# The last modulation vector of an adaLN block: one ScalarE scaling and a chain of accumulating DMAs in the place of VectorE sums and two matmuls

## The chip, the cores and the metric

The kernel runs on one core of one Trainium2 chip. The metric is the device time of one execution in microseconds (us). The kernel before ran three times: 440.43, 440.69 and 441.95 us, median 440.69 us. A separate execution was taken with the hardware profiler.

## The reference

One adaLN block on x of 2048 tokens by D = 448 channels, float32. Six modulation vectors of 448 numbers come from one matrix product; the last one, `gb`, is the subject of this document.

```python
mod = (_silu(c) @ w_mod).reshape(c.shape[0], 6, 1, -1)
sa, ca, ga, sb, cb, gb = (mod[:, 0], ..., mod[:, 5])
h = _layernorm(x) * (1 + ca) + sa
x = x + ga * _A_ref(h, A_wqkv, A_wo)        # linear attention, 16 heads of 28
h = _layernorm(x) * (1 + cb) + sb
x = x + gb * _B_ref(h, B_w1, B_b1, B_w2, B_b2)
```

`_B_ref` is a token-mixing MLP: layernorm, a product over the 2048 tokens with w1 (2048 by 1792), a gelu, and a product with w2 (1792 by 2048), each with a bias. `gb` multiplies what the MLP returns, so it is wanted only after the first of its two large products.

## The kernel before

**Layout.** Tokens are cut into 16 tiles of 128 rows (`NT`). Every float32 product is done as two or three fp32r matmuls: an operand is split into a high part (ScalarE copy) and a low part (VectorE subtraction, or a ScalarE negated copy followed by an accumulating DMA issued by GpSimd, as in `split_to`, `low` and `a_pk_parts`).

**Stages in program order.** After a start-up part, the loop `for t in range(3, NT)` (line 594) is the *first token stage*: for each token tile it projects keys, builds the high and low parts of phi(k), and adds to the 448 by 448 product `cacc` (line 453). Behind it stand the short middle parts: the sums `zs` and `zp` (lines 664 to 669), `csum`, `kvb` (line 691), `wp` (line 846) and the rows of `wp`, copied by SyncE DMAs (line 718). The loop `for i in range(NT + LAG)` (line 855) is the *second token stage*: it applies attention to tile i (`tq` line 758, `op` line 778), normalizes, and from i = 5 on runs the first steps of the w1 product (`up`, lines 828 to 830). The rest of the w1 product and the w2 product (`y`, lines 1028 and 1029) follow.

**Order and queues.** The schedule is written out by hand (`manual_schedule`): each engine runs its instructions in program order, so a waiting instruction holds up all that is behind it on the same engine. SyncE (SP) issues the loads in one such order, and GpSimd (POOL) issues the accumulating DMAs between its own small vector operations.

**Buffers.** Most tiles live in one pool of 76 buffers (`slot`, `NSLOT`); some in a pool of 25 (`tslot`, `NTOK`). A load whose buffer isn't free yet waits on SP, with all later loads behind it. Loads of w1 pieces (`pr`, `load_to`, line 242) run ahead of their splitting (`ph` and `pl`, `split_to`).

**The modulation vectors.** `sc` holds silu(c) as 112 rows by 4 columns. Vector j needs four tiles of w_mod (`load_mod`, line 113: 112 rows by 448), each scaled by one column of `sc`, added up, and then summed over the 112 rows. `mod_part` does the scaling and adding (ScalarE for the first piece of vector 5, line 179, VectorE for the other three, line 183). `mod_split` cuts the sum into high and low parts. `mod_sum2` multiplies both with a matrix of ones (lines 199 and 200), which sums over the rows and puts the result on all 128 partitions at once, and `mod_out` copies it out of PSUM (line 161).

For vector 5, `gb`, the four loads are issued at i = 12 of the second token stage, `mod_part` runs at i = 13, 14 and twice at 15, the matmuls at i = 16. Its readers come later: the multiplication of the gelu's result (`act`, line 945) and the bias term (lines 1155 and 1171).

Of the kernel before, what the change touches and what calls it, by code (L numbers as in the profile page):

```python
# [8 lines left out]
F32 = mybir.dt.float32  # L9
F32R = mybir.dt.float32r  # L10
AF = mybir.ActivationFunctionType
ALU = mybir.AluOpType
AX = mybir.AxisListType

P = 128
S, D, F = 2048, 448, 1792
NT = S // P
NF = F // P
G = 112
# [15 lines left out]
PRE2 = {16: (1, 0), 12: (1, 1), 8: (1, 2), 3: (4, 3), 1: (4, 4)}  # L35
MOD_AT = {11: [(4, 0)], 12: [(4, 1)], 13: [(4, 2)], 14: [(4, 3)], 15: [(3, 0), (3, 1)]}
QS = {0: 2, 4: 2}
WARM = 9
ACT_STATS = ()
PRE = 9  # L40
# [7 lines left out]
def block_kernel(ctx: ExitStack, tc: tile.TileContext, x, wqkv, wo, w1, b1, w2, b2, c, wmod, out):  # L48
    nc = tc.nc
# [5 lines left out]
    cst = ctx.enter_context(tc.tile_pool(name="cst", bufs=1))  # L55
# [9 lines left out]
    def slot(name, w=D, dt=F32, parts=P):  # L65
        return slots.tile([parts, w], dt, name=name, tag="slot", padded_shape=[P, 512])
# [41 lines left out]
    wm = {}  # L108

    def load_mod(j):  # L110
        for k in range(4):
            wm[j, k] = (tslot if j == 5 else slot)(f"wm{j}_{k}", parts=G)
            nc.sync.dma_start(wm[j, k], wmod[k * G:(k + 1) * G, j * D:(j + 1) * D])

    raw_w = {}
# [38 lines left out]
    nc.vector.tensor_scalar_add(ec, ec, 1.0)  # L154
    nc.vector.reciprocal(ec, ec)
    nc.vector.tensor_mul(sc, ct, ec)
    mods, macc, part = {}, {}, {}

    def mod_out(j, ps):
        mods[j] = cst.tile([P, D], F32, name=f"mod{j}")  # L160
        nc.scalar.activation(mods[j], ps[:, :D], AF.Copy, bias=1.0 if j in (1, 4) else 0.0)
# [13 lines left out]
    def mod_part(j, k):  # L175
        if k == 0:
            macc[j] = (tslot if j == 5 else slot)(f"acc{j}", parts=G)
            if j == 5:
                nc.scalar.activation(macc[j], wm[j, 0], AF.Copy, scale=sc[:, 0:1])
            else:  # L180
                nc.vector.tensor_scalar_mul(macc[j], wm[j, 0], sc[:, 0:1])
        else:
            nc.vector.scalar_tensor_tensor(macc[j], wm[j, k], sc[:, k:k + 1], macc[j], op0=ALU.mult, op1=ALU.add)
# [7 lines left out]
    def mod_split(j):  # L191
        acc = macc.pop(j)
        macc[j] = (moving(slot, f"mh{j}", parts=G), moving(slot, f"ml{j}", parts=G))
        split(acc, *macc[j])

    def mod_sum2(j):
        ps = bank(f"modp{j}")
        hi, lo = macc.pop(j)
        nc.tensor.matmul(ps[:, :D], ones_r[:G, :], hi, start=True, stop=False)
        nc.tensor.matmul(ps[:, :D], ones_r[:G, :], lo, start=False, stop=True)  # L200
        return ps

    Whi, Wlo = {}, {}

# [28 lines left out]
    raws, parts = {}, {}  # L233
    done = {"load": 0, "split": 0}

    def load_to(i):
        while done["load"] < min(i, len(pieces)):
            k = done["load"]
            src, r, c0, n = pieces[k]
            raws[k] = slot(f"pr{k}", 4 * P)  # L240
            rows = 1 if n == 4 else 2
            nc.sync.dma_start(raws[k].rearrange("p (r c) -> p r c", r=rows),
                              src[r * P:(r + rows) * P, c0 * P:(c0 + n) * P].rearrange("(r p) c -> p r c", p=P))
            done["load"] += 1

    def split_to(i):
        while done["split"] < min(i, len(pieces)):
            k = done["split"]
            if k in TOKP:
                hi, lo = tslot(f"ph{k}", F32R, w=4 * P), tslot(f"pl{k}", F32R, w=4 * P)  # L250
            else:
                hi, lo = slot(f"ph{k}", 4 * P, F32R), slot(f"pl{k}", 4 * P, F32R)
            if k in PIECE_DMA:
                full = raws.pop(k)
                nc.scalar.activation(hi, full, AF.Copy)
                nc.scalar.activation(lo, hi.bitcast(F32), AF.Copy, scale=-1.0)
                nc.gpsimd.dma_start(lo, full, accum_op=ALU.add)
            else:
                split(raws.pop(k), hi, lo)
            parts[k] = (hi, lo)  # L260
            done["split"] += 1
# [332 lines left out]
    for t in range(3, NT):  # L594
        kp = project(t, 1, "kp")
        if t + 1 < NT:
            a_transpose(t + 1)
        a_outer(t - KV_LAG)
        if t in Q_EARLY:
            a_q(t)  # L600
        if t == 10:
            mp = mod_sum2(2)
        if t + 1 < NT:
            a_split(t + 1)
        if t + 2 < NT:
            a_norm_a(t + 2)

        for j, i in MOD_AT.get(t, ()):
            mod_part(j, i)
        if 11 <= t < 15:  # L610
            nc.vector.tensor_mul(wo_sb[t - 11], wo_sb[t - 11], mods[2][:G])
        a_exp(t, kp)
        if t + 2 < NT:
            a_norm_b(t + 2)
        a_pk(t, kp)
        a_phi_q()
        a_pk_parts(t - 1)
        if t + 3 < NT:
            a_stats(t + 3)
        if t + 2 < NT:  # L620
            a_dup(t + 2)
        if t == 3:
            a_high(3)
            a_high(4)
        if t + 2 < NT:
            a_high(t + 2)
        if t == 10:
            mod_out(2, mp)
        if t + 4 < NT:
            load_x(t + 4)  # L630
        if 5 <= t < 9:
            mod_part(2, t - 5)
        if t == 9:
            mod_split(2)
        if 5 <= t <= 5 + QLATE:
            phi_q_sum(t - 5)
        if t in (10, 11):
            load_mod(14 - t)
        if t == 4:
            for g in range(4):  # L640
                w = tslot(f"wo{g}", parts=G)
                nc.sync.dma_start(w, wo[g * G:(g + 1) * G, :])
                wo_sb.append(w)
            load_qkv(2, tslot)
            b1c = cst.tile([P, NF], F32, name="b1c")
            nc.sync.dma_start(b1c, b1.rearrange("(k p) -> p k", p=P))
            b2c = cst.tile([P, NT], F32, name="b2c")
            nc.sync.dma_start(b2c, b2.rearrange("(k p) -> p k", p=P))
        load_to(PRE_LOAD.get(t, 0))
# [20 lines left out]
    mod_split(4)  # L670
    mod_split(3)
    load_to(14)
    split_to(4)
    zb = tslot("zb")
    nc.scalar.activation(zb, zp[:, :D], AF.Copy, bias=S * 1e-6)
# [18 lines left out]
    kvm = slot("kvm", parts=G)  # L694
    nc.vector.tensor_mul(kvm, kvb[:G, :D], mask)
    mod_out(4, mp)
    mp = mod_sum2(3)
    load_to(PRE + MID + 3)
    split_to(8)
# [104 lines left out]
    def b_mean2(t, i):  # L804
        nm2s[t] = small.tile([P, 1], F32, name=f"ny{t}", tag="ny")
        nc.gpsimd.tensor_scalar_mul(nm2s[t], sums.pop(t), -1.0 / D)
        b_square(ys[t], nm2s[t], b_sums(i)[:, 1:2], f"b{t}")
# [36 lines left out]
    for g in range(4):  # L844
# [5 lines left out]
        Wph.append(hi)  # L850
        Wpl.append(lo)
    mod_out(3, mp)

    accs, early = None, []
    for i in range(NT + LAG):
        if i == NT - 4:
            load_mod(5)
        if NT - 3 <= i < NT:
            mod_part(5, i - NT + 3)
        if i < NT:  # L860
            b_transpose(i)
        if 0 <= i - 1 < NT:
            b_out(i - 1)
        nq = min(len(late), QS.get(i, 1))
        for _ in range(nq):
            a_q(late.pop(0))
        t = i - LAG
        mp = mod_sum2(5) if i == NT else None
        if t >= 0:
            if t == 0:  # L870
                accs = [bank(f"up{f}") for f in range(4)]
            if i > NT:
                if not early:
                    early = [bank(f"up{W1G[1][0] + f}") for f in range(W1G[1][1])]
                r = i - NT - 1
                step(NT + r, early, H2h[r], H2l[r], r == 0, False)
            step(t, accs, H2h[t], H2l[t], t == 0, t == NT - 1)
        if mp is not None:
            mod_out(5, mp)
        scale, res, norm1, norm2 = i + 1 < NT, 0 <= i - 2 < NT, 0 <= i - 3 < NT, 0 <= i - 4 < NT  # L880
        if i < NT:
            b_high(i)
        if res:
            b_res(i - 2)
        if scale:
            b_prod(i + 1)
        if norm2:
            b_norm2(i - 4, i)
        if res:
            b_mean1(i - 2, i)  # L890
        if norm1:
            b_norm1_a(i - 3)
        if scale:
            b_sum(i + 1)
        if norm1:
            b_norm1_b(i - 3, i)
        if scale:
            b_eps(i + 1)
        if i < NT:
            b_low(i)  # L900
        if norm1:
            b_mean2(i - 3, i)
        if scale:
            b_recip(i + 1)
        if scale:
            b_scale(i + 1)
        if scale:
            b_dup(i + 1)
        if norm2:
            b_low2(i - 4)  # L910
        a_phi_q(nq)
        load_to(14 + (i + 1) // 2)
        if res or norm1:
            b_rstd(i, 0 if res else 1, 2 if norm1 else 1)
        if i == NT - 1:
            mod_part(5, 3)
            mod_split(5)
        split_to(10 + (i + 1) // 2)


# [291 lines left out]
```

## Time and profile before

| | |
|---|---|
| median of three runs | 440.69 us (440.43 to 441.95) |
| profiled execution, its own device time | 440.77 us |
| span of the profiled execution, first to last instruction | 439.1 us |
| PE (TensorE) busy in the span | 433.9 us, 99% |
| DVE (VectorE) busy | 365.1 us, 83% |
| ACT (ScalarE) busy | 266.9 us, 61% |
| POOL (GpSimd) busy | 119.3 us, 27% |
| granted TensorE clock | 1.0 throughout |

Times inside the execution are counted in us from the first instruction. The columns of a timeline are: start, duration, engine, line, operation, written tile <- read tiles, shapes, count, and in brackets the idle time of the engine before it with what ended it. "SPq" is the queue of DMA issues on SyncE. A row of the view of waits gives engine, line, what it waited for, then total us, number of waits and the longest. Matmuls overlap: a matmul's row lasts about 0.36 us, but the next one starts about 0.2 us after it, and that distance is what a matmul costs.

### The profile page before, as it was taken

The page shows a single profiled execution, that of the slowest core. Times are in us where ns is not written, and L with a number is a line of the kernel's source. Part 1 is how long each engine was busy: PE and PEld are TensorE (multiplying, and loading weights), DVE is VectorE, ACT ScalarE, POOL GpSimd, SP SyncE. Part 2 cuts the span into 40 slices and gives each one's busy share as a digit, 9 for nine tenths or more (in the row PEclk, how much of TensorE's full clock was granted, in tenths as well). Part 3 has the DMA queues.
Part 4 walks back from the last instruction along what each step waited for, and adds up shares of the span by engine and source line. Part 5 has one row for each costly group of instructions (what it writes and reads, how often), then busy time and mean ns, then how long its engine had stood idle before and what let it go on. Part 6 is the DMA issues. An engine that isn't in the chain of part 4 may idle for free.

```text
span 439.1 us, 7288 instructions
## 1 busy us (share of the span) xinstructions
PE 433.9 (99%) x2394; PEld 402.4 (92%) x2394; DVE 365.1 (83%) x792; ACT 266.9 (61%) x570; POOL 119.3 (27%) x196
## 2 busy tenths in 40 slices
PE   8999999999999999999999999999999999999996
PEld 7689999999899999999999999999999999999996
DVE  5996898988898999997469586439999998898894
ACT  3778877655657777776766254236675555655550
POOL 2205775520024455664300000010112230231110
PEclk9999999999999999999999999999999999999999
DMA  8987999993441224222427546476667977977531
GB/s 233 303 213 117 181 197 230 221 258 102 138 100 26 47 47 123 50 50 60 132 69 237 177 143 186 131 194 187 151 143 191 177 172 176 188 161 208 75 52 34
DMA packets 65022, 64.51 MB, mean 147 GB/s; under 512 B 8472, under 2 KB 56792, under 8 KB 64984
## 3 DMA queue, kind: packets, MB, share of 16 engines
q1 hardware_dynamic: 54608, 47.62, 36.8%
q0 software_dynamic: 10368, 16.42, 23.8%
q8 instruction: 19, 0.31, 0.3%
q14 instruction: 19, 0.16, 0.1%
q10 hardware_dynamic: 8, 0.00, 0.0%
HBM read 41.88 MB, written 7.34 MB: 112 GB/s over the span
## 4 chain that ended last, share of the span: by engine, by line
PE 95%; DMA 3%; DVE 1%; ACT 0%; issue 0%; SPq 0%; DVEq 0%
PE y L1028 19%; PE up L829 10%; PE up L828 10%; PE up L830 10%; PE y L1029 9%; PE op L778 8%; PE cacc L453 8%; PE qp L356 7%; PE kp L356 7%; DMA wl<-wr 2%; PE tq L758 2%; PE tp L325 1%; DMA wm<-in_w_mod_dram 1%; PE kvb L691 1%; PE wp L846 1%; PE colp L475 0%
## 5 line engine op out<-in xcount | busy, mean ns | idle before, releaser
L829 PE MATMUL up<-h2l,ph 128*128 128x448 f32 x224 | 81.3, 363 | 0.0
L828 PE MATMUL up<-h2h,ph 128*128 128x448 f32 x224 | 81.2, 362 | 0.0
L830 PE MATMUL up<-h2h,pl 128*128 128x448 f32 x224 | 80.7, 360 | 0.0
L988 POOL DMA_DIRECT2D a<-a x16 | 14.1, 948 | 145.5 <-DMA a<-in_B_w_dram 97.8
L828 PEld LDWEIGHTS up<-h2h,ph 128*128 128x128 f32 x224 | 42.0, 188 | 3.3
L830 PEld LDWEIGHTS up<-h2h,pl 128*128 128x128 f32 x224 | 41.9, 187 | 3.0
L829 PEld LDWEIGHTS up<-h2l,ph 128*128 128x128 f32 x224 | 42.0, 188 | 2.1
L80 DVE TENSOR_TENSOR pl<-pr,ph 128x512 fp32r<-128x512 f32 x48 | 32.3, 686 | 11.5 <-ACT ph L79 8.6
L79 ACT ACTIVATE ph<-pr 128x512 fp32r<-128x512 f32 x48 | 29.1, 627 | 17.8 <-PE up L829 7.4
L1050 ACT ACTIVATE cc<-y 128x448 f32<-128x448 f32 x24 | 13.0, 544 | 22.9 <-PE y L1029 22.9
L453 PE MATMUL cacc<-pkh,xh 128*128 128x448 f32 x64 | 24.3, 379 | 0.0
L453 PE MATMUL cacc<-pkl,xh 128*128 128x448 f32 x64 | 23.2, 363 | 0.0
L778 PE MATMUL op<-oh,pth 128*128 128x448 f32 x60 | 23.0, 383 | 0.0
L1071 POOL DMA_DIRECT2D out_dram<-yt x14 | 12.9, 921 | 34.9 <-DVE yt L1057 25.4
L778 PE MATMUL op<-oh,ptl 128*128 128x448 f32 x60 | 21.7, 362 | 0.0
L356 PE MATMUL qp<-wh,hh 128*128 128x448 f32 x60 | 21.6, 365 | 0.0
L356 PE MATMUL qp<-wh,hl 128*128 128x448 f32 x60 | 21.4, 362 | 0.0
L356 PE MATMUL kp<-wh,hl 128*128 128x448 f32 x56 | 20.3, 363 | 0.0
L356 PE MATMUL kp<-wh,hh 128*128 128x448 f32 x56 | 20.2, 362 | 0.0
L736 POOL TENSOR_SCALAR den<-den 128x16 f32<-128x16 f32 x16 | 8.6, 536 | 39.2 <-DVE den L733 39.1
L763 ACT ACTIVATE pth<-tq 128x512 fp32r<-128x512 f32 (+1 forms) x16 | 9.6, 599 | 15.7 <-PE tq L758 15.6
L302 POOL TENSOR_TENSOR rs<-ve,mhalf 128x1 f32<-128x1 f32 x16 | 13.9, 869 | 18.8 <-DVE ve L300 18.5
(234 smaller groups left out, 1356.9 us busy)
## 6 DMA issues: line engine op xcount, KB each, us to landing
pr<-in_B_w_dram SPq DMA_DIRECT2D x56, 256.0 KB, 2.9
a<-in_B_w_dram SPq DMA_DIRECT2D x32, 256.0 KB, 4.3
a<-in_B_w_dram SPq DMA_DIRECT2D x32, 192.0 KB, 4.2
wm<-in_w_mod_dram SPq DMA_DIRECT2D x24, 196.0 KB, 4.9
x<-in_A_x_dram SPq DMA_DIRECT2D x16, 224.0 KB, 4.0
out_dram<-x SPq DMA_DIRECT2D x14, 224.0 KB, 2.0
out_dram<-yt POOLq DMA_DIRECT2D x14, 224.0 KB, 4.5
pk<-pk POOLq DMA_DIRECT2D x12, 224.0 KB, 4.7
```

What stands on the lines that cost most here:

```text
L79: nc.scalar.activation(hi, full, AF.Copy)
L80: nc.vector.tensor_sub(lo, full, hi.bitcast(F32))
L302: nc.gpsimd.tensor_tensor(rs, ve, mhalf[:, 0:1], op=ALU.pow)
L356: nc.tensor.matmul(o, a[:, ch * P:(ch + 1) * P], b, start=(n == 0), stop=(n == 10))
L453: nc.tensor.matmul(cacc[ch][:, :D], a[:, s], b, start=(t == 0 and i == 0), stop=(t == NT - 1 and i == len(todo) - 1))
L778: nc.tensor.matmul(opb[t][:, :D], a[:, g * P:(g + 1) * P], b, start=(n == 0), stop=(n == len(todo) - 1))
L828: nc.tensor.matmul(ps[:, :D], hi[:, sl], mh, start=first, stop=False)
L829: nc.tensor.matmul(ps[:, :D], hi[:, sl], ml, start=False, stop=False)
L830: nc.tensor.matmul(ps[:, :D], lo[:, sl], mh, start=False, stop=last)
L988: nc.gpsimd.dma_start(w, a, accum_op=ALU.add)
L1028: nc.tensor.matmul(ps[:, :D], h[:, s], w, start=opens and r == r0, stop=False, skip_group_check=True)
L1029: nc.tensor.matmul(ps[:, :HD], l[:, s], wh, start=False, stop=closes and r == PAIRS - 1 - (LAST if (q, m) == (NP - 1, 6) else 0), skip_gro ...
```

## The change

- **Loads.** The four tiles of w_mod for vector 5 are loaded at t = 12 of the first token stage instead of i = 12 of the second, ahead of the w1 pieces of that place, and lie in the pool of 76 instead of the pool of 25.
- **Scaling.** ScalarE scales the four tiles in place: two at t = 14 and two at t = 15.
- **Sum.** Ten accumulating DMAs, all issued by GpSimd, do the additions. At t = 15 tile 2 is added to tile 0 and tile 3 to tile 1; after `mod_split(3)` tile 1 is added to tile 0. Then seven folds each add the lower half of the remaining rows to the upper half: 112 rows to 56 after `mod_out(4)`, 56 to 28 after `mod_out(3)`, and 28 to 14, 7, 4, 2 and 1 at i = 3 to 7 of the second token stage. Each needs the one before.
- **Spreading.** SyncE writes the one row to DRAM at i = 9 and reads it back onto all 128 partitions at i = 10.
- **Removed.** For vector 5: three VectorE multiply-adds, the split, two matmuls and their PSUM bank, and the ScalarE copy out of PSUM.

```diff
+FOLD_AT = {3: 28, 4: 14, 5: 7, 6: 4, 7: 2}
...
-            wm[j, k] = (tslot if j == 5 else slot)(f"wm{j}_{k}", parts=G)
+            wm[j, k] = slot(f"wm{j}_{k}", parts=G)
...
+    def mod_fold(j, n):
+        acc = macc[j]
+        h = (n + 1) // 2
+        nc.gpsimd.dma_start(acc[:n - h], acc[h:n], accum_op=ALU.add)
+
+    def mod_row(j):
+        mrow[j] = park.tile([1, D], F32, name=f"mrow{j}")
+        nc.sync.dma_start(mrow[j], macc.pop(j)[:1])
+
+    def mod_rows(j):
+        mods[j] = cst.tile([P, D], F32, name=f"mod{j}")
+        nc.sync.dma_start(mods[j], mrow[j].to_broadcast([P, D]))
...
+        if t == 12:
+            load_mod(5)
+        if t in (14, 15):
+            for k in (2 * t - 28, 2 * t - 27):
+                nc.scalar.activation(wm[5, k], wm[5, k], AF.Copy, scale=sc[:, k:k + 1])
+        if t == 15:
+            for k in range(2):
+                nc.gpsimd.dma_start(wm[5, k], wm[5, k + 2], accum_op=ALU.add)
...
     mod_split(3)
     load_to(14)
+    nc.gpsimd.dma_start(wm[5, 0], wm[5, 1], accum_op=ALU.add)
+    macc[5] = wm[5, 0]
...
     mod_out(4, mp)
+    mod_fold(5, G)
...
     mod_out(3, mp)
+    mod_fold(5, 56)
...
-        if i == NT - 4:
-            load_mod(5)
-        if NT - 3 <= i < NT:
-            mod_part(5, i - NT + 3)
...
-        mp = mod_sum2(5) if i == NT else None
...
-        if mp is not None:
-            mod_out(5, mp)
...
         if norm1:
             b_mean2(i - 3, i)
+        if i in FOLD_AT:
+            mod_fold(5, FOLD_AT[i])
+        if i == 9:
+            mod_row(5)
+        if i == 10:
+            mod_rows(5)
...
-        if i == NT - 1:
-            mod_part(5, 3)
-            mod_split(5)
```

More of the change, by code (lines that the diff above doesn't have):

```diff
@@ L156, in block_kernel @@
     nc.vector.tensor_mul(sc, ct, ec)
-    mods, macc, part = {}, {}, {}
+    mods, macc, part, mrow = {}, {}, {}, {}
     def mod_out(j, ps):
```

## The prediction

> **What bounds the kernel now.** I read the page first, then what PE waited for, then the busy time by stage.
>
> ```profile
> span 439.1 us, 7288 instructions
> PE 433.9 (99%) x2394; PEld 402.4 (92%) x2394; DVE 365.1 (83%) x792; ACT 266.9 (61%) x570; POOL 119.3 (27%) x196
> ...
> PE 95%; DMA 3%; DVE 1%; ACT 0%; issue 0%; SPq 0%; DVEq 0%
> ```
>
> ```profile
> PE warm L143 <- DVE mhalf L97: 1.1, 1, 1.1
> PE tp L489 <- DVE xn L515: 0.4, 1, 0.4
> ```
>
> ```profile
> 94.00:125.00 31.00, 31.00 (x170) 27.75 (x169) 25.52 (x46) 18.74 (x39) 0.81 (x3) 1.00 0.49 148
> 125.00:205.00 80.00, 80.00 (x426) 74.50 (x425) 74.88 (x179) 58.16 (x124) 44.20 (x91) 1.00 0.25 56
> 205.00:425.00 220.00, 220.00 (x1256) 207.94 (x1255) 177.48 (x376) 121.67 (x259) 30.83 (x43) 1.00 0.63 158
> ```
>
> The chain that ended last is 95% PE; PE's only two listed waits, 1.5 us in all, lie in the start-up; and in the three stages that the change touches PE is busy for the whole stretch. (Columns of the last fence: stretch, its length, then busy time and count of PE, weight loads, DVE, ACT and POOL, then the granted clock.) So TensorE's own stream sets the end. Taking work from PE shortens the run by what that work occupies; work taken from or given to other engines counts only once PE has to wait. The upside is therefore small and known, the downside is any new wait of PE.
>
> **The change part by part.** *Two matmuls go.*
>
> ```profile
> 203.78 0.37 PE L199 MATMUL modp<-mh,ones_r 112*128 112x448 f32 x1
> 203.98 0.37 PE L200 MATMUL modp<-ml,ones_r 112*128 112x448 f32 x1
> 204.19 0.37 PE L828 MATMUL up<-h2h,ph 128*128 128x448 f32 x1
> ```
>
> From the start of the first to the start of the next other matmul: 204.19 - 203.78 = 0.41 us. That is the whole gain on the path. The VectorE multiply-adds, the split and the copy out of PSUM that also go are hidden behind PE's full stretch; I count them as nothing.
>
> *Four scalings on ScalarE.* Two come at t = 14, two at t = 15. Their price is that of the same form at the start of the kernel, the L165 row; the timeline of ScalarE shows where they fall.
>
> ```profile
> L165 ACT ACTIVATE acc<-wm,sc x2: 668/668/668, 4.2 to 7.9; 112x448 f32<-112x448 f32 x2
> ```
>
> ```profile
> 94.45 0.55 ACT L363 ACTIVATE ek<-kp 128x448 f32<-128x448 f32 x1 [2.48 <-PE kp L356]
> ...
> 96.70 0.58 ACT L427 ACTIVATE pkh<-pk 128x448 fp32r<-128x448 f32 x1 [0.81 <-DVE pkl L429]
> 97.19 1.14 ACT L79 ACTIVATE ph<-pr 128x512 fp32r<-128x512 f32 x2
> ```
>
> The first two, 1.34 us, fit into the 2.48 us that ScalarE idles before 94.45. The last two start when it falls idle at 96.70 - 0.81 = 95.89 and end by 97.23, so `pkh` of the last tile comes up to 0.53 us late, and VectorE, which waits for it, hands that on to `zl`:
>
> ```profile
> 103.02 0.62 DVE L80 TENSOR_TENSOR zl<-pk,zh 128x448 fp32r<-128x448 f32 x1 [0.70 <-ACT zh L79]
> ```
>
> ```profile
> 105.45 0.36 PE L669 MATMUL zp<-zl,ones_r 128*128 128x448 f32 x1
> ```
>
> `zl` ends at 103.64, its matmul starts at 105.45: 1.81 us of cover against 0.53. Cost nothing; without that cover, 0.53.
>
> *Four loads move ahead of the w1 pieces.* SP issues one load when a buffer comes free, so the four take the places of four pieces.
>
> ```profile
> SPq L242 <- DMA xl<-h: 7.3, 1, 7.3
> ```
>
> ```profile
> 82.52 18.95 SPq L242 DMA_DIRECT2D pr<-in_B_w_dram  x14
> ...
> 89.53 1.40 SPq L242 DMA_DIRECT2D pr<-in_B_w_dram  x2
> ...
> 109.36 0.37 SPq L242 DMA_DIRECT2D pr<-in_B_w_dram  x1
> 115.56 0.57 SPq L718 DMA_DIRECT2D oh<-wph  x1
> 149.07 20.26 SPq L242 DMA_DIRECT2D pr<-in_B_w_dram  x3
> 169.38 1.83 SPq L113 DMA_DIRECT2D wm<-in_w_mod_dram  x4
> ```
>
> ```profile
> pr<-in_B_w_dram SPq DMA_DIRECT2D x56, 256.0 KB, 2.9
> wm<-in_w_mod_dram SPq DMA_DIRECT2D x24, 196.0 KB, 4.9
> pk<-pk POOLq DMA_DIRECT2D x12, 224.0 KB, 4.7
> pl<-pr POOLq DMA_DIRECT2D x8, 256.0 KB, 3.4
> wl<-wr POOLq DMA_DIRECT2D x1, 224.0 KB, 8.1
> oh<-wph SPq DMA_DIRECT2D x1, 28.0 KB, 2.3
> ```
>
> The first piece then goes out with the fifth issue, at 89.53, and lands 2.9 us later at 92.4; ScalarE wants it at 97.19. The w_mod tiles themselves, issued from 82.52 on and within the four places before 89.53, land 4.9 us after that, by 94.4 at the worst, and their scalings come at 92 to 96. Behind the last load of this group SP turns to the copies of `wp`, which wait for other work until 115.56; the group ended at 109.36 + 0.37, which leaves 5.8 us for the four places. The bound on the other side is the slot rival below. Later on 1.83 us of SP's time at 169.38 comes back, which nothing needed.
>
> *Ten accumulating DMAs on POOL.* The pair is issued behind the last scaling, at 97.23 and about 98.1, one issue costing about 0.94 us (L257, below). With the 4.7 us of the `pk` row it has landed at 102.8, the third at 107.5, and the fold of 112 rows is issued by 108.5. Behind it on POOL stands `den` of the first tile:
>
> ```profile
> 114.71 0.29 POOL L736 TENSOR_SCALAR den<-den 128x16 f32<-128x16 f32 x1 [23.05 <-DVE den L733]
> ...
> 159.30 0.23 POOL L806 TENSOR_SCALAR ny<-sy 128x1 f32<-128x1 f32 x1
> 160.40 0.19 POOL L811 TENSOR_SCALAR vw<-vs 128x2 f32<-128x2 f32 x1 [0.88 <-ACT sqb L285]
> ...
> 163.57 0.65 POOL L736 TENSOR_SCALAR den<-den 128x16 f32<-128x16 f32 x1 [0.24 <-DVE den L733]
> ```
>
> POOL idled 23.05 us there: 6.2 us of cover are left. Were every link as slow as the worst row, 8.1 us, that fold would be issued by 115.2 and `den` be 0.5 us late.
>
> The folds at i = 3 to 7 stand between `ny` and `vw`. At i = 7 POOL idles 0.88 us at that place and again 0.24 us before the `den` of a later tile, which `pn`, and then PE's transpose, wait for:
>
> ```profile
> L257 POOL DMA_DIRECT2D pl<-pr x8: 894/944/970, 126.5 to 203.5; - x8
> ```
>
> ```profile
> 165.54 0.20 DVE L751 COPY pn<-pn 128x64 f32<-128x64 f32 x1
> ```
>
> ```profile
> 161.10 0.27 PE L758 MATMUL tq<-ident,pn 128*128 128x128 f32 x1
> 166.16 0.38 PE L758 MATMUL tq<-ident,pn 128*128 128x128 f32 x2
> ```
>
> One issue of 0.94 us overruns the 0.88 by 0.06; cover behind that is 0.24 + (166.16 - 165.74) = 0.66 us. The fold before was issued one token step, 166.16 - 161.10 = 5.06 us, earlier, and needs 3.4 us to land by the row of the same stage. So: nothing, and small folds should be cheaper still.
>
> Here a rule speaks against the change. The Trainium skill (SBUF — State Buffer, section SBUF: two separate sides) says that a VectorE copy from SBUF to SBUF in fp32 keeps GpSimd from writing the descriptors of its DMAs, and gives about 3.1 us instead of 0.62 for one; by that difference, an estimate of 2.5 us from this page, each of the five folds could hold up POOL and the time would be some 9 us longer. This trace doesn't show it: eight issues in that stage, where VectorE is busy 94%, lie between 0.894 and 0.970 us, and the only such copy of a token step lasts 0.20 us.
>
> *The row and its spreading.* At i = 9 SP waits for the last fold (issued about 160.5, landed about 164), then 2.3 us for the write and up to 4.9 for the read: `gb` is there at about 171. It is first read at 224.9; the piece that queues behind the two on SP is read after 201.77.
>
> ```profile
> L945 DVE TENSOR_TENSOR u<-u,mod x14: 614/618/626, 224.9 to 314.8; 128x448 f32<-128x448 f32 x14
> ```
>
> ```profile
> 201.77 0.62 ACT L255 ACTIVATE ph<-pr 128x512 fp32r<-128x512 f32 x1
> ```
>
> **Sum.** The profiled execution took 440.77 us (439.1 of span and 1.67 around it); 440.77 - 0.41 = 440.36. It stands 0.08 above the median of the runs, so against the 440.69 the forecast is 440.28, say 440.3 us.
>
> **The rivals.**
>
> *The gain is given back (440.7).* 0.41 us is kept only if everything behind arrives 0.41 us earlier too. For it: VectorE is busy 94% of the second token stage, and the slack of `pn` there was 0.42 us. Against: VectorE loses work at that very place, and PE shows no wait at all after the start.
>
> *A buffer that comes free too late (442.8, the other side).* The pool of 76 is tight: following each buffer from first to last use in program order, I count 71 in use around the last key tile, and the four new ones, two of them freed only by the landing of the pair, make it 73 or more just where SP already waited 7.3 us for a buffer. If ScalarE's `ph` at 97.19 is given a buffer that the pair frees, it starts at 102 instead: 4.8 us late in the worst case, and `zl` with it. PE's `zp` has 1.81 us of cover, so PE loses 3.0 us: 440.3 + 3.0 = 443.3, or 442.8 where the pair lands within 4.2 us, between the rows' 3.4 and 4.7. It decides from 2.2 us of lateness on. Against: engines other than SP waited for no transfer there.
>
> *The folds hold POOL (445).* If a fold waits for the one before, `vw`, `nb` and `den` wait behind it. It decides once a fold lands later than 5.06 - 0.94 + 0.88 + 0.66, about 5.7 us, after its issue. At the 8.1 us of the `wl` row each of the four links that wait for one another (i = 4 to 7) costs 8.1 - 5.7 = 2.4 us; with two of the four so slow the time is 440.3 + 4.8 = 445. For it: the 8.1 row. Against: that one is of the start-up, and the 3.4 row is of this stage. The skill's rule above would act through the same queue.
>
> **How the numbers follow.** Forecast 440.3: 0.62. Given back, 440.7: 0.18. Late buffer, 442.8: 0.12. POOL held: 0.05. The rest, 0.03, is for something that I don't see, evenly to both sides. About 0.5%, 2.2 us, is what a measurement of this kernel can tell from no change. Faster by more would need 438.5: PE has only 5.2 us without work in the whole span, in start-up and tail that the change doesn't touch, so 0.03. Slower by more means above 442.9: half of the late buffers, the POOL case and the unseen, 0.13. Within: 0.84. The range goes from 439.7 (the forecast less the scatter of the runs below their median and some more) to 442.6, up to the late-buffer case; for the likeliest alone it is 439.9 to 441.0.
>
> **What would show it.** Right: two PE matmuls fewer, PE without waits from 94 to 425 us, the ten POOL issues at about 1 us or less, `den` at about 114.7, the `gb` row landed by 175. The late buffer would show as ScalarE or VectorE waiting for a DMA into `wm` at 96 to 105 and PE waiting at `zp`; the POOL case as `vw` or `den` waiting for a DMA and PE idle before `tq`; the given-back gain as an equal PE span with some PE wait behind 204. A time outside 439.7 to 442.6, or a PE wait above 0.5 us in the stretch of the folds, makes the prediction wrong.

## The result, and the profile after

The changed kernel took 443.52 us, median of six runs (442.62 to 444.26); the kernel before on the same chip 441.22 us (440.43 to 441.95). The ratio is 1.0055, 95% interval [1.0042, 1.0068]: slower by 2.3 us, where 0.4 us less was forecast. The profiled execution took 442.62 us.

From the page of the changed kernel, the span, the busy times and the chain of waits:

```profile
span 440.9 us, 7306 instructions
...
PE 433.9 (98%) x2392; PEld 401.7 (91%) x2392; DVE 362.7 (82%) x788; ACT 267.9 (61%) x571; POOL 126.4 (29%) x206
...
PE 87%; DMA 7%; issue 2%; DVE 2%; POOL 1%; ACT 1%; SPq 0%; DVEq 0%; POOLq 0%
```

PE has two instructions fewer and is busy for the same 433.9 us, in a span that is 1.8 us longer. The chain was 95% PE and 3% DMA; now it is 87% and 7%. So PE waited for something, and a transfer is part of it. What PE waited for, in the changed kernel:

```profile
PE kvb L715 <- DVE cs L704: 1.4, 1, 1.4
PE warm L144 <- DVE mhalf L98: 1.1, 1, 1.1
PE tp L503 <- DVE xn L529: 0.6, 1, 0.6
PE qp L370 <- DMA wl<-wr: 0.3, 1, 0.3
```

The last three lie in the start-up, where the kernel before shows two of them too, and where single executions differ by some tenths. The first is new. By stage, the changed kernel:

```profile
94.00:125.00 31.00, 29.61 (x161) 26.29 (x160) 24.71 (x46) 18.33 (x38) 4.80 (x7) 1.00 0.69 179
125.00:205.00 80.00, 80.00 (x426) 74.52 (x425) 74.84 (x178) 58.85 (x125) 47.17 (x95) 1.00 0.25 54
```

The second token stage, where five of the folds run, is as full as before: 80.00 of 80.00 us. The middle part isn't: 29.61 of 31.00. Most of the loss is there. Its timeline on PE, changed kernel:

```profile
109.02 0.95 PE L715 MATMUL kvb<-cs,wr 128*112 128x112 f32 x8
111.36 2.61 PE L715 MATMUL kvb<-cs,wr 128*112 128x112 f32 x24 [1.39 <-DVE cs L704]
```

and in the kernel before:

```profile
108.26 3.31 PE L691 MATMUL kvb<-cs,wr 128*112 128x112 f32 x32
```

`kvb` multiplies the four tiles `cs`. Two of them are copied by VectorE (line 704), and PE stops after eight matmuls because the first of these copies is late. The product starts 0.76 us later than before, and the first matmul behind it stands at 113.74, 2.40 us later than before (111.34): over `kvb` PE loses 1.64 us. VectorE's timeline in the changed kernel says why:

```profile
106.78 0.68 DVE L81 TENSOR_TENSOR pl<-pr,ph 128x512 fp32r<-128x512 f32 x1
110.08 0.69 DVE L81 TENSOR_TENSOR pl<-pr,ph 128x512 fp32r<-128x512 f32 x1 [2.62 <-DMA wm<-wm]
110.69 1.15 DVE L704 COPY cs<-cacc 128x448 f32<-128x448 f32 x2
```

`pl` is the low part of a w1 piece and has nothing to do with the modulation vector. Yet it waits 2.62 us for a DMA between two `wm` tiles, and the copies to `cs` queue behind it. What the two can share is a buffer: `pl` writes into a buffer of the pool of 76 that one of the new tiles held (the runs with single tiles in memory of their own, below, test this). POOL's timeline in the changed kernel names the transfer:

```profile
98.81 1.73 POOL L660 DMA_DIRECT2D wm<-wm  x2 [5.67 <-ACT wm L657]
105.90 0.83 POOL L695 DMA_DIRECT2D wm<-wm  x1 [5.36 <-DMA wm<-wm]
110.29 0.86 POOL L207 DMA_DIRECT2D wm<-wm  x1 [3.56 <-DMA wm<-wm]
117.13 0.29 POOL L761 TENSOR_SCALAR den<-den 128x16 f32<-128x16 f32 x1 [5.99 <-DVE den L758]
```

The third add (line 695, tile 1 into tile 0) goes out at 105.90. `pl` starts at 110.08 and the fold of 112 rows, which needs the sum, at 110.29: both were released by that landing. Tile 1 has its last reader in this add, so its buffer is handed on when the add has landed.

There is a smaller loss some 15 us earlier. ScalarE in the changed kernel, behind the last key tile:

```profile
91.71 0.60 ACT L80 ACTIVATE hh<-tp 128x512 fp32r<-128x512 f32 x1 [1.76 <-DMA pk<-pk]
...
93.52 1.24 ACT L657 ACTIVATE wm<-wm,sc 112x448 f32<-112x448 f32 x2
```

and the same operation in the kernel before:

```profile
90.03 0.60 ACT L79 ACTIVATE hh<-tp 128x512 fp32r<-128x512 f32 x1 [0.31 <-PE tp L325]
```

`hh` starts 1.68 us later and waits for the landing of an accumulating DMA on `pk`. It doesn't read `pk`, so this too is a buffer that it is given, though one of the stage's own, and what is new is that the landing is late. PE, which needs `hh` for `kp`, has no idle time to show for it in this profile, but runs its first `kp` matmuls further apart: it is 0.21 us behind the kernel before at the last matmul ahead of them (92.06 against 91.85) and 0.76 us at the fourth of them (93.40 against 92.64). That is 0.55 us. ScalarE, and VectorE behind it, stay late from here on: the first `pl` above starts at 106.78, in the kernel before at 104.63. Between 82 and 94 us the DMA engines (the last two numbers of a row are their mean busy share and GB/s) stand so, kernel before:

```profile
82.00:94.00 12.00, 12.00 (x65) 11.20 (x64) 11.43 (x25) 6.73 (x15) 6.49 (x8) 1.00 1.07 241
```

The share is above 1 already. The prediction quoted the next stage, 94 to 125 us with 0.49, and not this one, into which it put four loads of 196 KB. What SP issues from 82 to 89 us, in the changed kernel and then in the kernel before:

```profile
82.43 1.98 SPq L114 DMA_DIRECT2D wm<-in_w_mod_dram  x4
84.58 4.53 SPq L256 DMA_DIRECT2D pr<-in_B_w_dram  x4
```

```profile
82.52 3.99 SPq L242 DMA_DIRECT2D pr<-in_B_w_dram  x4
```

Eight loads instead of four: the new ones did not take the places of w1 pieces, they came on top of them.

Two theories came from this. **Theory B, hand-over:** a buffer of the new tiles comes free only when a DMA lands, and a compute engine is given it. **Theory T, crowd:** the four loads, issued from 82 us on, lengthen the landings of the first stage's own transfers (`pk`, `pkl`, `xl`), for which its engines wait. Against them stood **theory A**, that the scalings and adds cost the time in the first stage by themselves, and **theory F**, that the accumulating DMAs cost the second token stage something.

### The profile page after: what moved, and what is told of

It is laid out like the page before. It is cut to its first block, busy times and chain, and to the rows that moved or that the text cites. A ratio compares the mean times of both kernels' runs of the same rounds, so it can differ in the third digit from the quotient of the medians.

```text
span 440.9 us, 7306 instructions
## 1 busy us (share of the span) xinstructions
PE 433.9 (98%) x2392; PEld 401.7 (91%) x2392; DVE 362.7 (82%) x788; ACT 267.9 (61%) x571; POOL 126.4 (29%) x206
## 4 chain that ended last, share of the span: by engine, by line
PE 87%; DMA 7%; issue 2%; DVE 2%; POOL 1%; ACT 1%; SPq 0%; DVEq 0%; POOLq 0%
PE y L1050 19%; PE up L855 10%; PE up L854 10%; PE up L853 10%; PE y L1051 9%; PE op L803 8%; PE qp L370 6%; PE kp L370 5%; PE cacc L467 4%; DMA wm<-wm 2%; DMA wl<-wr 2%; DMA pk<-pk 2%; PE tq L783 2%; PE tp L339 1%; DMA wm<-in_w_mod_dram 1%
## 5 line engine op out<-in xcount | busy, mean ns | idle before, releaser
L967 DVE TENSOR_TENSOR u<-u,mod 128x448 f32<-128x448 f32 x14 | 8.7, 620 | 12.9 <-ACT u L966 12.6
```

## The experiments

All ratios are medians against the kernel before on the same chip, with 95% intervals; diffs are against the changed kernel unless said otherwise. A ratio of 0.001 is 0.44 us here. Profiles are single executions, and their start-up alone differs: the matmuls at about 26 us stand up to 0.7 us earlier or 0.5 us later than in the kernel before.

### Four tiles in memory of their own

```diff
+    def own(k):
+        if k in (0, 3):
+            return mod_tile(5 if k == 0 else 3)[:G]
+        return cst.tile([P, D], F32, name=f"own{k}")[:G]
-            wm[j, k] = slot(f"wm{j}_{k}", parts=G)
+            wm[j, k] = own(k) if j == 5 else slot(f"wm{j}_{k}", parts=G)
```

(`mod_tile` gives the tile that holds vector j later on.)

> The change, with the four w_mod tiles in buffers of their own outside the pool of 76 (two new ones, and those of the vectors 5 and 3, which are empty until later). Loads, scalings, ten accumulating DMAs and order stay. Theory B (the four tiles make the pool too tight; others wait for buffers that a transfer frees): the 1.4 us wait of PE at kvb and the 0.4 us at kp are gone, and the two matmuls' 0.41 us is left as gain: ratio to before 0.999 (0.9975 to 1.0005). Theory S (the four scalings delay ScalarE), theory F (the accumulating DMAs hold GpSimd) and theory T (the transfers of the early loads delay other transfers): as the change, ratio 1.005, PE still waits at kvb.

Measured: 440.78 beside 440.91 us, ratio 0.9995 [0.9985, 1.0006]. SP's timeline in this kernel:

```profile
73.74 0.47 SPq L124 DMA_DIRECT2D mod<-in_w_mod_dram  x1
74.25 1.20 SPq L124 DMA_DIRECT2D own<-in_w_mod_dram  x2
```

The loss against the kernel before is gone, with the scalings and all ten accumulating DMAs where they were. That rules out theory A as the main cause. But the edit did two things: no buffer is handed on, and the loads, which no longer wait for a buffer, went out 8 us earlier. B and T are still mixed.

The expected gain is missing, though: the run without vector 5, at the end, gives 0.9981, so about 0.6 us may still be lost here (the two intervals just touch). The profile shows a candidate, a wait of PE for `h` of 0.8 us at about 84 us. `h` waits 1.39 us for `rs`, which GpSimd computes behind this add on `pk`:

```profile
82.54 0.84 POOL L462 DMA_DIRECT2D pk<-pk  x1 [2.40 <-issue]
```

It goes out 0.3 us after the `pk` add issued at 73.83 has landed. That one took 8.4 us beside the early loads; the longest `pk` add issued between 70 and 95 us took 6.4 us in the kernel before. This looks like theory T at an earlier place.

### The kernel before with 72 buffers

```diff
-NSLOT, NTOK = 76, 25
+NSLOT, NTOK = 72, 25
```

> The kernel before, with 72 buffers in the pool in the place of 76 and nothing else changed. Theory B: a wait of PE between 90 and 112 us into the run, 1 to 3 us in all, without any scaling, accumulating DMA or early load: ratio 1.002 to 1.007. Theories S, F and T: ratio 1.000 (0.9985 to 1.0015).

Measured: 441.48 us, 1.0016 [1.0004, 1.0029], and no wait of PE between 90 and 112 us in its profile. (The profile is of one of the fastest executions, 440.80 us.) A tighter pool costs something, but not visibly in this place: four buffers fewer are not the same as four buffers that a late DMA frees.

### Tile 1 alone, and tiles 2 and 3 alone, in memory of their own

```diff
+            wm[j, k] = own(k) if j == 5 and k in (1,) else slot(f"wm{j}_{k}", parts=G)
```

> The change, with tile 1 alone in a buffer of its own; tiles 0, 2 and 3 stay in the pool. In the changed kernel a VectorE subtraction (pl, line 81) took over the buffer that tile 1 gives up when the third add has landed, and waited 2.6 us for it. Theory B: that wait and the 1.4 us of PE at kvb are gone, the 0.4 us at kp may stay: ratio 1.000 (0.999 to 1.002). Theories S, F and T: ratio 1.005.

Measured: 441.60 us, 1.0017 [1.0004, 1.0029]. The wait at `kvb` is gone, as theory B has it. In this profile, which is of the slowest execution of this kernel (442.99 us), another stands in its place:

```profile
PE cacc L477 <- DMA pkl<-pk: 1.5, 2, 1.3
```

With tiles 2 and 3 instead (`k in (2, 3)`):

> The change, with tiles 2 and 3 in buffers of their own, tiles 0 and 1 in the pool. Theory B: the buffer of tile 1 is still handed on when the third add lands, so a VectorE or ScalarE instruction between 105 and 111 us can wait for that transfer: ratio between that of tile 1 alone (1.0017) and that of the change (1.0055), about 1.003. Theory T: as that of tile 1 alone, 1.0017, since the transfers are the same.

Measured: 442.56 beside 440.85 us, 1.0037 [1.0023, 1.0052], and the wait stays:

```profile
PE kvb L725 <- DVE cs L714: 1.0, 1, 1.0
```

So the wait at `kvb` follows tile 1's buffer, the one that the third add frees. The changed kernel a second time, in the same group of runs:

> The changed kernel itself, beside the others on one chip. Ratio 1.0055 (1.004 to 1.007), PE waiting at kvb for a VectorE copy that stands behind a subtraction which waits for the third add.

```profile
PE kvb L715 <- DVE cs L704: 1.5, 1, 1.5
```

It gave 443.46 us, 1.006 [1.0041, 1.008]: time and wait both repeat.

### Own memory, but the loads held to 82 us

Against the first experiment:

```diff
+        if t == 11:
+            hold += [own(k) for k in range(4)]
+            for h in hold:
+                nc.vector.memset(h[:, 0:1], 0.0)
```

> As the run with four buffers of their own, but the four early loads are held back, by a one-column VectorE fill of each at t = 11, until about the place where they went out in the changed kernel (82 us), so that their transfers crowd the same stretch. Theory B (buffers alone): no wait of PE at kvb or kp, ratio 0.9995 (0.9985 to 1.0005). Theory T (the crowded transfers make the pkl, xl and pk DMAs land late): PE waits for pkl between 90 and 98 us, 0.5 to 1.5 us, ratio 1.001 to 1.004.

Measured: 442.59 beside 440.85 us, 1.0033 [1.0021, 1.0045]. No buffer is shared, and the only thing beside the one-column fills (0.06 to 0.07 us each in the profile) that differs from the first experiment is when the loads go out. The w1 pieces behind them start at 84.17, against 83.77 there, so it is not the pieces that come late. SP's timeline, the stretch from 82 to 94 us, the landings of `pkl` issued between 80 and 95 us, and what PE waited for:

```profile
81.74 0.31 SPq L124 DMA_DIRECT2D mod<-in_w_mod_dram  x1
...
84.17 7.50 SPq L266 DMA_DIRECT2D pr<-in_B_w_dram  x6
```

```profile
82.00:94.00 12.00, 11.16 (x60) 10.15 (x59) 10.97 (x23) 8.58 (x19) 5.76 (x7) 1.00 1.04 256
```

```profile
DMA to landing us min/median/max: 3.9/6.9/7.7
```

```profile
PE cacc L477 <- DMA pkl<-pk: 1.0, 2, 0.8
```

PE is busy 11.16 of 12.00 us there, against 12.00 in the kernel before (the first experiment's profile has 11.21, by its wait for `h`), and waits for `pkl`, whose DMA takes up to 7.7 us to land. In the kernel before, in the same view:

```profile
DMA to landing us min/median/max: 3.2/5.1/5.6
```

The engines' share did not rise (1.07 before, 1.04 here) and the bytes moved hardly did (241 and 256 GB/s), although four more loads were asked for; the landings became longer instead. That is theory T without theory B. The Trainium skill (DMA: Bandwidth & Descriptors, section Issuing engines are not separate DMA queues) says that DMAs run on the same 16 engines and interleave, whichever engine issued them; these rows agree, loads from SP lengthening POOL's adds from 5.6 to 7.7 us at the worst.

### The crowd alone, in the kernel before

Against the kernel before:

```diff
+        if t == 11:
+            for k in range(4):
+                extra.append(...)
+                nc.vector.memset(extra[k][:, 0:1], 0.0)
+        if t == 12:
+            for k in range(4):
+                nc.sync.dma_start(extra[k], wmod[k * G:(k + 1) * G, 5 * D:6 * D])
```

> The kernel before with four further loads of 196 KB at t=12, held to about 82 us by four one-column fills of VectorE as in the run with held loads, into memory that nothing else uses then; what they bring is not used, no scaling and no accumulating DMA is added, and the two matmuls of the fifth vector stay. Theory T (crowded transfers lengthen the landings on which the first stage waits): a wait of PE for pkl of 0.5 to 1.5 us as with held loads, and a ratio of 1.001 to 1.004. If the scalings and the adds in the first stage are the cause there, and not the loads (theory A): 1.000 (0.999 to 1.001) and no wait for pkl above the kernel before's.

Measured: 442.00 beside 440.75 us, 1.0028 [1.001, 1.0045]. What PE waited for, the stretch from 82 to 94 us, and the landings of `pkl` as above:

```profile
PE cacc L458 <- DMA pkl<-pk: 0.8, 2, 0.6
```

```profile
82.00:94.00 12.00, 11.70 (x61) 10.14 (x60) 11.23 (x29) 8.08 (x18) 6.81 (x8) 1.00 1.04 246
```

```profile
DMA to landing us min/median/max: 4.5/6.2/6.8
```

Four loads that nobody reads cost 1.2 us. This is theory T as expected, and without scalings or adds theory A has no part in it. Two reservations: the runs lie far apart (440.45 to 444.32 us), and of the 0.8 us for `pkl` the longer wait, 0.6, stands at 70 us, before the extra loads go out at 82.7. So the ratio carries this verdict more than the single profile does.

All profiles together show the mechanism more plainly. Take the last add on `pkl` of the stage, issued at about 88 to 90 us. In the six profiles with four w_mod loads issued between 81 and 86 us (the changed kernel twice, tile 1 alone, tiles 2 and 3 alone, held loads, crowd alone) it took 5.5 to 7.7 us to land; in the eight without them (the first experiment, the kernel before and all other versions here) 3.5 to 5.1 us.

### Everything moved into the second token stage

Load at i = 1, scalings at i = 4 and 5, adds at 5 and 6, folds at 7 to 13, row and spreading at 15 and 16; a second version three to four steps later.

```diff
+        if i == 1:
+            load_mod(5)
+        if i in (4, 5):
+            for k in (2 * i - 8, 2 * i - 7):
+                nc.scalar.activation(wm[5, k], wm[5, k], AF.Copy, scale=sc[:, k:k + 1])
...
```

> The change, moved to where fewer buffers are in use: loads at i = 1 of the second token stage, scalings at i = 4 and 5, the first three adds at i = 5 and 6, the seven folds at i = 7 to 13, the row at i = 15 and its spreading at i = 16. Theory B: no wait of PE, ratio 0.999 (0.9975 to 1.0005). Theory F: all ten accumulating DMAs now stand between the small operations of GpSimd in the stage where VectorE is busiest, so PE waits before tq, ratio above 1.003. Theory T: no early load in the crowded stretch, ratio 0.999 as under B.

Measured: 441.82 beside 440.91 us, 1.0016 [1.0006, 1.0026]. PE's wait, at 161 us, and POOL's timeline at the pair of adds of i = 5:

```profile
PE tq L772 <- DVE pn L757: 1.2, 1, 1.2
```

```profile
149.25 1.85 POOL L917 DMA_DIRECT2D wm<-wm  x2 [1.77 <-ACT wm L914]
151.17 0.66 POOL L825 TENSOR_SCALAR vw<-vs 128x2 f32<-128x2 f32 x1
```

Neither `kvb` nor the first stage loses anything now. The chain that ends in PE's wait, followed back, runs through GpSimd: it waits 1.77 us for the last scaling, spends 1.85 us on issuing the pair, and only then computes `vw`, on which the rest of the token step hangs, down to `pn`. VectorE's longest wait for an `rq`, 1.8 us at 143.6 us, which the next expectation names, stands behind the scalings of i = 4 and not of i = 5.

> As the late version, but loads at i = 4, scalings two each at i = 8 and 9, adds at i = 9 and 10, folds at i = 11 to 17, the row at i = 18 and its spreading at i = 19. In the late version VectorE's pq waited 1.8 us behind the scalings of i = 5, where the transpose had least slack, and PE lost 1.2 us before tq. If the place of the scalings was the cause: no wait of PE before tq, ratio 0.999 (0.998 to 1.0002), the gain of the two matmuls. If the accumulating DMAs on GpSimd are (theory F): PE waits before tq at i = 9 to 17, ratio above 1.001.

Measured: 442.05 beside 440.85 us, 1.0021 [1.0012, 1.0029], with a wait of 0.5 us at `tq` of about 176 us. Later is no better, and the chain of the wait runs through the same place: POOL waits 1.76 us for the last scaling of i = 9 and then issues the pair at 171.12, for 1.83 us. So in both profiles the pair directly behind the scalings is what PE waits for in the end; neither run tests it by itself.

### A lull for each part

The loads go into memory that holds finished vectors, and out at about 102 us, behind the pieces of the first stage. There the kernel before has a DMA share of 0.34:

```profile
98.00:110.00 12.00, 12.00 (x71) 11.33 (x70) 10.00 (x17) 7.03 (x16) 0.00 (x0) 1.00 0.34 106
```

All four scalings stand at about 112 us, the adds and folds at the start of the second token stage.

```diff
     load_to(14)
+    load_mod(5)
...
     split_to(8)
+    for k in range(4):
+        nc.scalar.activation(wm[5, k], wm[5, k], AF.Copy, scale=sc[:, k:k + 1])
...
     mod_out(3, mp)
+    for k in range(2):
+        nc.gpsimd.dma_start(wm[5, k], wm[5, k + 2], accum_op=ALU.add)
```

> The same sum over rows, built to meet neither the hand-over of a buffer nor the crowd of transfers at 82 to 92 us: the four tiles lie in memory that holds the gate and the first two modulation vectors and the third (free by then), the four loads go out behind the last raw tile of the first stage (about 102 us), ScalarE scales all four at about 112 to 115 us, where it idles, the pair of adds follows the shift's sum, the third add and the seven folds stand at i=1 to 8. If hand-over (theory B) and crowd (theory T) are the whole cause, only the gain of two matmuls (0.41 us) is left: a ratio of 0.999 (0.998 to 1.0005) and no wait of PE over 0.4 us between 90 and 205 us other than those of the kernel before. If the chain of accumulating DMAs costs the fused stage something wherever it runs, as the run with folds at i=11 to 17 suggests for late places (theory F, about 1 us), the ratio is 1.001 to 1.002.

Measured: 441.98 beside 440.75 us, 1.0033 [1.0019, 1.0047]: a miss. PE lost nothing up to 129 us and then this (timelines of PE, of SP and of POOL in this kernel):

```profile
130.16 0.44 PE L803 MATMUL op<-oh,pth 128*128 128x448 f32 x1 [0.78 <-DMA oh<-wpl]
```

```profile
116.92 1.81 SPq L743 DMA_DIRECT2D oh<-wph  x2
118.83 2.38 SPq L743 DMA_DIRECT2D ol<-wpl  x2
...
125.72 0.59 SPq L743 DMA_DIRECT2D oh<-wpl  x1
```

```profile
115.10 1.78 POOL L879 DMA_DIRECT2D mod<-mod  x2 [0.31 <-issue]
...
124.88 0.87 POOL L924 DMA_DIRECT2D mod<-mod  x1 [0.29 <-issue]
```

The pair of adds had moved to where SyncE copies the rows of `wp`. SP's issues of two copies took 1.81 and 2.38 us, and the last copy went out at 125.72 and was waited for until 130.16. From the chain of waits, the landing of that copy:

```profile
125.72 4.31 DMA oh<-wpl
```

It went out beside the third add, and took 4.31 us; no copy to `oh` took more than 2.6 us in the kernel before. The same theory T, in a stage that I had taken for empty.

### The same with the adds behind the copies

```diff
+        if i == 3:
+            for k in range(2):
+                nc.gpsimd.dma_start(wm[5, k], wm[5, k + 2], accum_op=ALU.add)
+        if i == 4:
+            nc.gpsimd.dma_start(wm[5, 0], wm[5, 1], accum_op=ALU.add)
```

with the folds at i = 5 to 11 and the row at i = 13 and 14.

> The version with loads at about 102 us, own memory and scalings at about 112 us, but with the pair of adds at i=3, the third add at i=4, the folds at i=5 to 11, the row at i=13 and its spreading at i=14, so that the pair and the first fold no longer run beside SyncE's copies of the split weights (115 to 126 us). If the 0.8 us wait of PE for the copy oh<-wpl at 129 us was all that the version before it lost (its PE stood +1.03 us against the kernel before from there on), this one is at 440.1 to 440.6 beside 440.75, a ratio of 0.999 (0.998 to 1.0005), without a wait for oh. If the pair and the fold, wherever they lie in the fused stage, lengthen a transfer that is waited for (theory F), a wait of 0.3 to 1.2 us stands at another tile behind 129 us, and the ratio is 1.001 to 1.003.

Measured: 440.41 us (439.81 to 440.80) beside 441.04 us (440.37 to 442.38), ratio 0.9983 [0.9974, 0.9992]. This version beats both kernels. SP's timeline at the same copies:

```profile
117.10 1.18 SPq L743 DMA_DIRECT2D oh<-wph  x2
118.37 1.18 SPq L743 DMA_DIRECT2D ol<-wpl  x2
...
124.08 0.59 SPq L743 DMA_DIRECT2D oh<-wpl  x1
```

The copies go out in 1.18 us again, the last one 1.64 us earlier than in the version before it, and PE has no wait behind the start-up. The last `op` matmul ahead of the two removed ones stands at 203.54 (203.57 in the kernel before) and the first matmul behind them at 203.75 (204.19): nothing is lost on the way, and 0.41 us is won. Theory F, that accumulating DMAs cost the second token stage something wherever they lie, falls with it: pair, third add and seven folds all run there and cost nothing that shows. What the two late versions had and this one has not is a pair issued directly behind its scalings; since this version also moved the loads and the memory, that this alone was their loss stays an inference.

### The gain alone

The kernel before without the loads, the scaling and the two matmuls of vector 5 (the third vector stands in for it, so the gate of the MLP is left out of the computation).

```diff
     mod_out(3, mp)
+    mods[5] = mods[3]
-        mp = mod_sum2(5) if i == NT else None
```

> The kernel before without the fifth vector's work: no loads, no scaling, no two matmuls; the third vector stands in its place (this leaves out a part of the computation: the MLP gate is not computed). It measures the gain alone, the most that any placement of the replaced sum could bring. By the two matmuls at 203.78 and 203.98 us: 0.41 us, a ratio of 0.9991 (0.998 to 0.9998). If these two matmuls were covered by something else behind them, 1.000.

Measured: 440.19 beside 441.04 us, 0.9981 [0.9971, 0.9991]. That is all that any replacement could win, and the version before has it. The interval, 0.4 to 1.3 us, touches the 0.41 us of the two matmuls at its lower end; the median, 0.85 us, is above it. The profile says which part is the change's: PE stands 0.26 us ahead of the kernel before at the last matmul ahead of the two (203.31 against 203.57), nearly all of it from the start-up, and 0.68 us at the first one behind them (203.51 against 204.19). So the two matmuls give 0.42 us, and VectorE's lighter load adds nothing that shows; the rest of the median is not explained by this profile.

## Why the prediction was wrong

**What bounds the kernel.** Right: TensorE's stream sets the end, and only a wait of PE costs time. But "in the three stages that the change touches PE is busy for the whole stretch" left out a fourth stretch, 82 to 94 us, where the loads run. PE is just as full there (12.00 of 12.00 us); what would have told is the last-but-one number of its row, the DMA share of 1.07.

**Two matmuls, 0.41 us.** Right in place; 0.41 lies at the low end of what the run without vector 5 measured, 0.4 to 1.3 us, and its profile has 0.42 us at that place. The changed kernel earned it too, behind the waits that ate it: the matmul that stands at 204.19 before comes at 206.17, 1.98 us later, and the first one behind `kvb` still came 2.40 us later (113.74 against 111.34). So the rival of a gain given back behind 204 us is refuted as well.

**Four scalings, cost nothing.** Their price was right, in the changed kernel:

```profile
L657 ACT ACTIVATE wm<-wm,sc x4: 653/666/680, 93.5 to 98.3; 112x448 f32<-112x448 f32 x4
```

against 668 ns forecast. In the first experiment they run at the same place in the program, and all that it can still lose, by medians, is the 0.6 us or so between its 0.9995 and the 0.9981 of the run without vector 5.

**Four loads, "the four take the places of four pieces": this step failed.** They took no places: SP issued eight loads from 82 to 89 us instead of four, and the first piece went out at 84.58, not at 89.53. Why buffers for all eight were free the runs do not show. The step asked when the pieces and the tiles would land, from medians of the queue rows, and never what the loads would do to the transfers that were already there: the term for that stood at nothing without a reason. The row of 82 to 94 us with a DMA share of 1.07 was not read. The crowd alone cost 1.2 us in the kernel before (1.0028), and own memory with the loads held at 82 us came out at 1.0033.

**The slot rival: right in its mechanism, wrong in place and price.** It gave 0.12 to a buffer that a DMA frees too late for a compute engine, through ScalarE's `ph` at 97.19, freed by the pair, with PE losing 2.5 to 3.0 us at `zp`. It was VectorE's `pl`, freed by the third add, with PE waiting 1.4 us at `kvb`, some 10 us later than named. The step had followed tiles 2 and 3 and not tile 1, which is freed one add later, and it judged by who waited for a transfer before the change instead of by who takes the next buffer. That its 442.8 lies only 0.7 below the measured median is luck: the loss over `kvb` was 1.64 us and not 2.5, the crowd's cost came on top, and the kernel before itself stands at 441.22 in six runs, not at the 440.69 of the three that the forecast started from.

**Ten accumulating DMAs on POOL.** The chain was later than its sum, since it starts late and lands slowly: the fold of 112 rows went out at 110.29 instead of 108.5, and the cover held; `den` waited for VectorE, not for POOL. The folds cost what was forecast or less:

```profile
L207 POOL DMA_DIRECT2D wm<-wm x7: 843/867/914, 110.3 to 161.9; - x7
...
DMA to landing us min/median/max: 2.0/2.2/4.3
```

867 ns instead of 0.94 us, and landed in 2.2 us at the median instead of 3.4. The rival that the folds hold POOL is refuted for this kernel: five folds lie in a stage where PE is busy 80.00 of 80.00 us. In the two late versions POOL did hold `vw` up, not by a fold that waits for the one before it but by the pair that waits for its scalings. The rule of VectorE starving descriptor writes (the Trainium skill, SBUF — State Buffer, section SBUF: two separate sides; about 3.1 us for such a DMA), which the prediction set against the change, is not shown here either, with issues of 0.914 us at the most and landings of 2.2 us at the median.

**The row and its spreading.** Right; the row went out at 164.02, and the spreading in the changed kernel:

```profile
165.23 0.33 SPq L215 DMA_DIRECT2D mod<-mrow  x1
```

Both are out 60 us ahead of the first reader.

**The sum and the range.** Two causes together made up the loss, against a gain of 0.42 us. The hand-over is the more regular one: over `kvb` PE lost 1.64 us in the changed kernel's profile and 1.73 us in the profile of its second measurement (0.56 us late at its start, 108.82, and 2.29 us late behind it, 113.63), and tile 1 in memory of its own brought the ratio from 1.0055 to 1.0017, 1.7 us. The crowd cost 0.55 us at `kp` in the first of these profiles. In the second PE waits there:

```profile
PE kp L370 <- ACT hh L80: 0.5, 1, 0.5
```

With the slower matmuls behind that wait it lost 1.07 us (from 0.51 us ahead, 91.34 against 91.85, to 0.56 us late, 93.20 against 92.64). Together that is 1.8 and 2.4 us net, beside the 2.3 us measured. What the crowd costs differs from version to version and from run to run: 1.2 us in the kernel before, 1.7 us net (about 2.2 with the gain) with held loads, and the twelve runs with the crowd alone spread over 3.9 us. What decides that is not settled. The range ended at 442.6, just under the price of the late buffer alone, and had no term for the crowd.

## What to carry to other kernels

Before a transfer is added or moved, read the DMA share of the stretch in which it will run, from issue to landing, and not only its engine's idle time: with a share near 1 the loads added here made other landings longer, and the engine that waited for one paid. The share alone is no verdict: the first experiment's loads went out from 73.74 us on, in a stretch with a share of 0.99 before the change (70 to 82 us), and cost little or nothing in the median. Ask as well whose landings in that stretch are waited for, and with how much slack. When a tile's last reader is a DMA, its buffer comes free with the landing, so follow that buffer to its next owner, or give such tiles memory that nothing else is waiting for. Moved into three lulls (loads where the share was 0.34, scalings where ScalarE idled, adds behind the copies), the same change came out 0.17% faster instead of 0.55% slower, of which 0.42 us, 0.1%, is in the trace.

## What the runs showed of the hardware that was not expected

- The landing time of one and the same DMA depended on what ran beside it. The 224 KB adds of `pkl` issued between 80 and 95 us took 3.2 to 5.6 us in the kernel before, and up to 7.7 us with four more loads of 196 KB beside them, at about the same DMA share (1.07 and 1.04).
- A wait of PE cost more than the idle time listed for it: 1.64 us for 1.39 at `kvb`, and 1.10 us for 0.84 at `cacc` in the profile with held loads. Listed idle time begins at the end of a row, some 0.16 us behind the point where the next matmul would have started, and in the second case the first matmul behind the wait was followed after 0.31 us (91.78, 92.09) instead of 0.2.
- SP's issues got longer while POOL's transfers ran: with the pair of adds in flight, SP needed 2.38 us for two copies that take it 1.18 us otherwise (one profile).
- A fold of 1 to 56 rows by an accumulating DMA costs POOL as much as an add of 112 rows, 843 to 914 ns against 829 to 1087 ns, and lands in 2.2 us at the median (4.3 at the most); VectorE, busy 94% of the stage of the last five, didn't lengthen them.
